# First batch's q and k loaded by head pair, its value rows held back, and PSUM banks taken as they come free, in a planned attention and feed-forward kernel

## The chip, the cores and the metric

The kernel runs on one core of a Trainium2 chip. The metric is the device time of one execution in microseconds, as the median of three runs. The core's engines are called PE (TensorE: matmuls and transposes into PSUM), DVE (VectorE), ACT (ScalarE), POOL (GpSimd, which here casts a few tiles and issues most loads) and SP (SyncE, which here only issues DMAs). PSUM, PE's output memory, has eight banks of 128 partitions by 512 float32.

## The reference

The first half is sparse attention over 8 batches, 8 heads, 576 positions and 64 values per head. The first four heads attend to a local band of 32 positions, the other four to every 32nd position. The second half is a feed-forward layer over 4608 tokens of 512 values with 2048 hidden units.

```python
scores = (1.0 / np.sqrt(D)) * np.matmul(q, k.transpose(0, 1, 3, 2))
rel = pos[:, None] - pos[None, :]
mask_local = (rel >= 0) & (rel < 32)
mask_strided = (rel >= 0) & (pos[None, :] % 32 == pos[:, None] % 32)
scores = np.where(masks[None], scores, -1000000000.0)   # heads 0-3 local, 4-7 strided
attn = softmax(scores)
x = np.matmul(attn, v).transpose(0, 2, 1, 3).reshape(B * S, H * D)
h = x @ w_in
r = np.maximum(h, 0.0)
out = (s * (r * r) + b) @ w_out
```

## The kernel before, in words

**Tiles.** In a batch, attention works on four pairs of heads, `(b, m)`: `m` 0 and 1 are local (six tiles of 96 positions), `m` 2 and 3 strided (eight tiles of 72). A pair's steps on PE are: transposes of q and k into PSUM (`trans`, L405 for local pairs of the first two batches, L413 otherwise), from where ACT or DVE copies them to `qD_loc`, `kT_loc`, `qD_str`, `kTs`; scores (L533, in the first batch with a mask matmul L530 ahead of each); exponentials on ACT (L551); products with v (`av`, L590); a reciprocal and a multiplication into `x_nat` (L605, L616, or L611 on ACT); transposes of `x_nat` (L638) and a copy of them into `xT`. Pairs of heads share one index `mm = m % 2`, so `ql` and `kl`, the tiles of the local heads, hold pair 0 in their first half and pair 1 in their second.

**Feed-forward.** Tokens go in nine blocks `T` of 512. `ff1` (called F1 below, L883) makes 16 hidden tiles per block with four matmuls each, one per `xT` tile `ct`; ACT or DVE apply relu and square into `gT`; `ff2` (L941, and `ff2_seven`, L851, from block 3 on) multiplies by `w_out`. F1 of block 0 needs all four pairs of batch 0 and `w_in`.

**Who orders what.** The whole program is recorded by a planner before it is built: `Plan` keeps a clock `t`, a free time per engine and a table of when each thing is expected to be there. PE's steps are recorded in the order in which the planner thinks them ready; posted jobs (copies, exponentials, casts, loads) go to the engine that the planner thinks would finish them first, among those that the post names a cost for. The numbers for when loads land are written by hand. On the chip each engine works through its own list strictly in order, and waits on semaphores where the expectation was too early.

**PSUM.** The eight banks are named `t` (one), `s` (two), `a` (one), `f1` (two) and `f2` (two). `group_of` deals the banks' tags out to transposes (`t`), scores (`s`) and products (`a`) by a fixed rotation, and inside a tag a step takes the next bank in turn, so that it waits for exactly that bank. Where PE would have nothing to do in the head of the kernel, `keep_running` records filler matmuls (L1177).

**Loads of the first batch.** POOL issues, one after the other: `ql`, `kl` (288 KB each as stored), `qs`, `ks`, `vs` (each in two pieces of 64 and 8 rows). SP issues the identity, two pieces of the local heads' v (`stage_v`, L240, one piece of 144 KB per head, float32, into a part of `w_out_sb` that is not yet used), and the mask addends `negs`. Then SP waits: `after_landing` issues a copy of one element of `ql` (L1051), which must wait for the landing of `ql`, and behind it in SP's list stand the v pieces of heads 2 and 3, the masks and two scalars. POOL casts the v pieces to float16 into `v_loc` (`cast_v`, two casts per pair of heads), copies 32 rows of them (`rows_before`), and only then, behind a small copy that waits for `qs` (L1069), issues the three pieces of `w_in` (L307, 2 MB). Behind these in POOL's list stand the casts for heads 2 and 3, the first piece of `w_out` (L313), the next batch's q and k, the rest of `w_out`, and the next batch's v.

Of the kernel before, what the change touches and what calls it, by code (L numbers as in the profile page):

```python
# [9 lines left out]
FP16 = mybir.dt.float16  # L10
FP32 = mybir.dt.float32
# [4 lines left out]
class Plan:  # L16
# [9 lines left out]
    def __init__(self):  # L26
        self.t = 0.0
        self.done = {}
        self.pend = []
        self.free = {"A": 0.0, "V": 0.0, "P": 7000.0, "D": 0.0, "X": 0.0, "Y": 0.0}  # L30
        self.count = {}

    def ready_at(self, needs):
        if any(k not in self.done for k in needs):
# [6 lines left out]
    def flush(self):  # L41
        while True:
            best = None
            for p in self.pend:
                r = self.ready_at(p[0])
                if r is not None and r <= self.t and (best is None or r < best[0]):
                    best = (r, p)
            if best is None:
                return
            r, p = best  # L50
            self.pend.remove(p)
            eng = min(p[1], key=lambda e: max(self.free[e], r) + p[1][e])
            end = max(self.free[eng], r) + p[1][eng]
            self.free[eng] = end
            p[2](eng)
            for k in p[3]:
                if isinstance(k, Group):
                    k = ("rel", k.tag, k.n)
                soon = isinstance(k, tuple) and k[0] == "soon"
                self.done[k] = end + (6000.0 if soon else p[4] or self.LAT[eng])  # L60

    def step_ready(self, s):
        r = self.ready_at(s.needs)
        if r is None:
# [47 lines left out]
def kernel(  # L112
# [17 lines left out]
    PS = 512  # L130
# [115 lines left out]
    nc.vector.memset(part32, 1.0 / 32)  # L246
    nc.vector.memset(vl_stage[0:LPAD], 0.0)
    for i in range(2):
        nc.vector.memset(qD_loc[i], 0.0)
        nc.vector.memset(kT_loc[i][:, 0:LPAD], 0.0)  # L250
        nc.vector.memset(qD_str[i], 0.0)
    for i in range(NV):
        nc.vector.memset(v_loc[i][:, :, :, D:D + 1], 1.0)
# [4 lines left out]
    for tl in p_bufs[False]:  # L258
        nc.vector.memset(tl[:, 16 * SQ:], 0.0)

    loaded = {}
    paired = {}

    def load_qk(b):
        for name, src in (("q", q), ("k", k)):
            tl = inp.tile([LQ, NL], FP16, tag=name + "l", name=name + "l")
            loaded[b, name + "l"] = tl
            if b >= (QB_DMA if name == "q" else KB_DMA):

                dst = tl.rearrange("p (m t e d) -> p m e t d", m=2, t=LT, e=2)  # L270
                for h in range(4):
                    nc.gpsimd.dma_start(out=dst[:, h // 2, h % 2],
                                        in_=src[b, h].rearrange("(t p) d -> p t d", p=LQ))
            else:
                nc.gpsimd.dma_start(out=h4(tl), in_=view_l(src, b))
        for name, src in (("q", q), ("k", k)):
            if name == "k":
                ts = ks[b % 2]
            elif b < QS_DMA + 2:
                ts = inp.tile([SR, NS], FP16, tag="qs", name="qs")  # L280
            else:
                ts = loaded[b - 2, "qs"]
            if name == "k" and b in (2, 3) or name == "q" and b in (QS_DMA, QS_DMA + 1):
                nc.gpsimd.memset(ts[64:SR], 0.0)
            load_s(ts, src, b)
            loaded[b, name + "s"] = ts
# [47 lines left out]
    def cast_v(b, loc, mm, key):  # L334
        nt, np_, dst = (LT, 128, v_loc) if loc else (ST, SQ, v_str)

        def g(eng):
            src = vl_stage if loc else loaded[b, "vs"].rearrange(
                "p (h t d) -> p h t d", h=4, d=D)
            for h in range(2 * mm, 2 * mm + 2):  # L340
                copy_on(eng, out=dst[b % NV][0:np_, h, :, 0:D], in_=src[:, h])
        n = nt * D
        plan.post([key], {"P": 1000.0} if loc else {"A": 2 * (170 + 0.83 * n), "V": 540.0}, g,
                  [("cast", b, mm) if loc else ("in", "vs", b, mm)])
        if loc:
            rows_before(b, mm, ("cast", b, mm))

    def rows_before(b, mm, key):
# [5 lines left out]
        def g(eng):  # L354
# [4 lines left out]
    TB, SB, AB, F1B, F2B = 1, 2, 1, 2, 2  # L359
    HEAD_T = 2  # L360
    PE_MASK = 1
    ps = {tag: [psum.tile([128, PS], FP32, name=f"ps_{tag}{i}") for i in range(n)]
          for tag, n in (("t", TB), ("s", SB), ("a", AB), ("f1", F1B), ("f2", F2B))}

    taken = {"a": 0, "t": 0, "s": 0}

    def group_of(kind, b, m, q=False):

        t, a, f1, f2 = ("t", TB), ("a", AB), ("f1", F1B), ("f2", F2B)
        banks = {"a": [a], "t": [t], "s": [("s", SB)]}[kind]  # L370
        if b == 0:
            banks = {"a": [f2, f2, f1], "t": [t, a], "s": [("s", SB), ("s", SB), f1]}[kind]
        elif b == 1 and kind == "a":
            banks = [f1, f1, a]
        elif b >= KB_DMA and kind == "a":
            banks = [a, t]
        elif b == 1 and q:
            banks = [t, f2]
        taken[kind] += 1
        return Group(*banks[taken[kind] % len(banks)])  # L380

    def bank(group):
        return ps[group.tag][group.n % group.bufs]

    def pair_steps(b, m):

# [196 lines left out]
        def av(e, j, group):  # L583
# [13 lines left out]
            if j % per == per - 1:  # L597
# [467 lines left out]
    nc.sync.dma_start(out=b_sb, in_=moe_b.to_broadcast([128, 1]))  # L1065
# [96 lines left out]
    def keep_running(until):  # L1162

        ghz = 1.2 if plan.t < 6000 else 2.4
        n = min(int((until - 100.0 - plan.t) * ghz) - 20, 512) // 128
        for tag, bufs in (("f1", F1B), ("s", SB), ("f2", F2B)):
            k = ("rel", tag, plan.count.get(tag, 0) - bufs)
            if k[2] < 0 or plan.done.get(k, until) <= plan.t:
                break
        else:  # L1170
            return False
        if n < 1:
            return False
        out = ps[tag][plan.count.get(tag, 0) % bufs][:, 0:128 * n]
# [93 lines left out]
```

## Time and profile before

| | |
|---|---|
| median of 3 runs | 307.34 us (307.26 to 307.39) |
| the profiled execution | 307.34 us, of which the span of the trace is 305.6 us |
| PE busy | 297.7 us, 97% of the span |
| DVE, ACT, POOL busy | 215.6, 183.7, 93.9 us |
| DMA moved | 37.31 MB, mean 122 GB/s |
| filler matmuls (L1177) | 9.64 us busy, all before 25 us |

PE is busy nearly throughout, and the head of the kernel is the part where some of its work is filler. Matmuls are pipelined and their ends are modelled, so busy time on PE also covers some short waits. A line with one time is a start in microseconds from the span's start; a line with two is a start and a length.

### The profile page before, as it was taken

The numbers are of one execution on the slowest core, as the hardware profiler recorded it, in microseconds if no ns is written. First come the engines' busy times: TensorE is split into PE (matmuls) and PEld (weight loads), VectorE is DVE, ScalarE is ACT, GpSimd is POOL, SyncE is SP. The second block draws the span as 40 slices with busy tenths as digits, with TensorE's granted clock in tenths as the row PEclk, the third lists the DMA queues.
The fourth block names the chain that finished last, engine by engine and source line by source line (L and its number), as shares of the span: only waits on it lengthen the run. The fifth ranks groups of instructions, "written<-read, shape, count | busy, mean of one in ns | idle before, by whom it ended". The sixth has DMA issues, their size and how long they took to land.

```text
span 305.6 us, 6880 instructions
## 1 busy us (share of the span) xinstructions
PE 297.7 (97%) x2686; PEld 206.6 (68%) x2686; DVE 215.6 (71%) x479; ACT 183.7 (60%) x330; POOL 93.9 (31%) x136
## 2 busy tenths in 40 slices
PE   8899999999999999999999999999999999999995
PEld 3775645666655567777567776778888666766884
DVE  6575857799868678449897987688765366737563
ACT  1786756698957794768397945794525444444300
POOL 7572549910980491089106830000000000000000
PEclk9999999999999999999999999999999999999999
DMA  7999999999999699999999999704010200300223
GB/s 128 207 211 206 214 160 158 197 184 148 80 156 170 73 150 132 194 150 143 125 201 141 145 141 195 167 17 127 2 36 34 71 1 34 105 0 2 84 73 121
DMA packets 100795, 37.31 MB, mean 122 GB/s; under 512 B 80874, under 2 KB 97770, under 8 KB 100762
## 3 DMA queue, kind: packets, MB, share of 16 engines
q0 software_dynamic: 57200, 18.08, 58.8%
q1 hardware_dynamic: 43562, 18.78, 31.7%
q8 instruction: 21, 0.34, 0.5%
q14 instruction: 12, 0.10, 0.1%
HBM read 36.86 MB, written 10.32 MB: 154 GB/s over the span
## 4 chain that ended last, share of the span: by engine, by line
PE 88%; DMA 8%; POOL 1%; issue 1%; ACT 1%; DVE 1%; SPq 0%; POOLq 0%
PE ps_f L883 38%; PE ps_f L851 21%; PE ps_f L941 12%; DMA ql<-in_q_dram 6%; PE ps_s L533 5%; PE ps_a L590 3%; DMA w_out_sb<-in_v_dram 2%; PE ps_s L851 2%; PE ps_t L413 2%; PE ps_t L590 1%; PE ps_t L851 1%; PE ps_s L941 1%; PE ps_t L638 1%; POOL v_loc L317 1%; PE ps_a L851 1%
## 5 line engine op out<-in xcount | busy, mean ns | idle before, releaser
L883 PE MATMUL ps_f<-xT,w_in_sb 128*128 128x512 f16 (+4 forms) x696 | 148.1, 340 | 0.1
L910 ACT ACTIVATE u<-ps_f 128x512 f16<-128x512 f32 x138 | 81.6, 596 | 73.2 <-PE ps_f L883 71.7
L883 PEld LDWEIGHTS <-w_in_sb 128*128 128x128 f16 x704 | 71.5, 113 | 32.1 <-issue 0.2
L851 PEld LDWEIGHTS <-gT 128*128 128x128 f16 x512 | 49.1, 98 | 11.5
L920 DVE TENSOR_TENSOR gT<-u 128x1024 f16<-128x1024 f16 x50 | 34.4, 688 | 24.7 <-ACT u L910 24.2
L941 PE MATMUL ps_f<-w_out_sb,gT 128*128 128x512 f16 x176 | 47.9, 379 | 0.3 <-DVE gT L920 0.3
L851 PE MATMUL ps_f<-w_out_sb,gT 128*128 128x256 f16 x312 | 43.4, 273 | 0.0
L941 PEld LDWEIGHTS <-gT 128*128 128x128 f16 x192 | 17.2, 98 | 12.3 <-DVE gT L920 0.4
L616 DVE TENSOR_TENSOR x_nat<-ps_a,rec 72x256 f16<-72x256 f32 (+1 forms) x52 | 23.8, 457 | 0.6
L551 ACT ACTIVATE p_loc<-ps_s 128x384 f16<-128x384 f32 x46 | 20.9, 493 | 5.0 <-PE ps_s L533 4.0
L918 ACT ACTIVATE gT<-u 128x1024 f16<-128x1024 f16 x22 | 23.3, 1058 | 0.6
L551 ACT ACTIVATE p_str<-ps_s 72x432 f16<-72x432 f32 (+1 forms) x46 | 20.8, 483 | 1.9 <-PE ps_s L533 1.7
L295 POOL DMA_DIRECT2D v_loc<-in_v_dram x28 | 20.7, 757 | 3.5 <-DVE qD_loc L317 1.8
L590 PEld LDWEIGHTS <-p_str 72*128 72x128 f16 x256 | 15.5, 98 | 8.8 <-issue 1.1
L723 DVE TENSOR_TENSOR gT<-gT 128x1024 f16<-128x1024 f16 x28 | 18.5, 683 | 2.6 <-ACT gT L918 1.3
L851 PE MATMUL ps_f<-w_mix,gT 128*128 128x256 f16 x144 | 18.3, 273 | 0.0
L851 PEld LDWEIGHTS <-S 128*128 128x128 f16 x160 | 15.4, 98 | 3.4
L1012 POOL COPY gate<-kT 1x1 f16<-1x1 f16 x6 | 1.9, 322 | 42.7 <-DMA kT<-ks 42.7
L605 DVE RECIPROCAL rec<-ps_a 72x4 f32<-72x4 f32 (+1 forms) x52 | 9.1, 174 | 8.3 <-PE ps_a L590 8.2
L723 DVE TENSOR_TENSOR S<-gT 128x1024 f16<-128x1024 f16 x16 | 10.6, 687 | 5.6 <-PE ps_f L851 4.5
L300 POOL DMA_DIRECT2D v_str<-in_v_dram x16 | 13.2, 828 | 3.8 <-PE ps_f L883 1.8
L851 PE MATMUL ps_f<-w_mix,S 128*128 128x256 f16 x96 | 13.7, 272 | 0.0
(156 smaller groups left out, 418.4 us busy)
## 6 DMA issues: line engine op xcount, KB each, us to landing
out_dram<-o SPq DMA_DIRECT2D x34, 256.0 KB, 2.4
w_out_sb<-in_moe_w_out_dram POOLq DMA_DIRECT2D x4, 512.0 KB, 10.8
v_loc<-in_v_dram POOLq DMA_DIRECT2D x28, 72.0 KB, 7.0
ql<-in_q_dram POOLq DMA_DIRECT2D x6, 288.0 KB, 6.3
qs<-in_q_dram POOLq DMA_DIRECT2D x6, 288.0 KB, 5.6
ks<-in_k_dram POOLq DMA_DIRECT2D x6, 288.0 KB, 6.7
kl<-in_k_dram POOLq DMA_DIRECT2D x4, 288.0 KB, 8.0
kl<-in_k_dram POOLq DMA_DIRECT2D x16, 72.0 KB, 4.0
```

What stands on the lines that cost most here:

```text
L295: nc.gpsimd.dma_start(out=vl[LPAD:128, h, :, 0:D], in_=v_band(b, h))
L533: nc.tensor.matmul(out=st["s", g][0:nk, c:c + 2 * nq], lhsT=(st["k"][:, i * nq:i * nq + nk] if loc else st["k"][:, i, 0:SQ]), rhs=st["q"][ ...
L551: nc.scalar.activation(out=st["pw", g][0:nk, 0:2 * n * nq], in_=st["s", g][0:nk, 0:2 * n * nq], func=AF.Exp, scale=scale)
L590: nc.tensor.matmul(out=st["a"][:, j % per, :], lhsT=st["pw", g][0:nk, i * nq:i * nq + WIDE], rhs=vt[0:nk, 2 * mm + e, j, :])
L616: nc.vector.tensor_tensor(out=st["x"][:, j0:j0 + per, 64 * e:64 * e + 64], in0=st["pa", e, j][0:nq, 0:per, 0:D], in1=st["rec", e, j][0:nq, ...
L723: nc.vector.tensor_tensor(out=at(out), in0=at(x), in1=at(y), op=op)
L851: nc.tensor.matmul(out=gts[name, T, t][:, 0] if halves else gts[name, T][:, t], lhsT=lhs(k, t), rhs=rhs(k), start=fresh and k == 0 and (ha ...
L883: nc.tensor.matmul(out=gts["h", T, ft][:, lo:hi], lhsT=w_in_sb[min(ft // 4, 2)][:, ct].rearrange("p (c x l) -> p c l x", x=128, l=4)[:, ma ...
L910: nc.scalar.activation(out=u, in_=gts["h", T, ft], func=AF.Relu)
L918: nc.scalar.activation(out=g, in_=u, func=AF.Square)
L920: nc.vector.tensor_tensor(out=g, in0=u, in1=u, op=ALU.mult)
L941: nc.tensor.matmul(out=gts[id_], lhsT=gts[T][:, ft, ts * 128:(ts + 1) * 128], rhs=w_out_sb[:, ft, cols], start=(ft == 0), stop=(ft == NFT ...
```

## The change

Five things change.

1. `load_qk(0)` loads the local q and k of batch 0 in four pieces, by pair of heads: q of pair 0, k of pair 0, q of pair 1, k of pair 1 (144 KB each) in place of two transfers of 288 KB.
2. SP issues `negs` ahead of v, only one piece of v (head 0) at the start, and the other three behind the one-element copy, which now reads the second half of `ql` and so waits for the third of the four pieces.
3. The order of the memsets on DVE is changed. The hand-written landing times are changed to a table `AT`.
4. The planner's cost table for the strided v cast of batch 0 names POOL too (1500 ns).
5. A `Group` now names a set of banks, and a step takes the one of them that the planner expects free first. More banks are named for transposes of batches 1 and 2, for F1 of block 0 and for the fillers. `rec` takes one pool of 8 buffers.

```diff
@@ Plan.flush, Plan.step_ready, Plan.emit, Group
-                    k = ("rel", k.tag, k.n)
+                    self.banks[k.name] = end + self.LAT[eng]
+                    k = ("rel", k)
...
-            n = self.count.get(s.group.tag, 0)
-            if n >= s.group.bufs:
-                k = ("rel", s.group.tag, n - s.group.bufs)
-                if k not in self.done:
-                    return None
-                r = max(r, self.done[k])
+            free = [self.banks[x] for x in s.group.names if self.banks[x] is not None]
+            if not free:
+                return None
+            r = max(r, min(free))
...
-            s.group.n = self.count.get(s.group.tag, 0)
-            self.count[s.group.tag] = s.group.n + 1
+            free = [x for x in s.group.names if self.banks[x] is not None]
+            s.group.name = min(free, key=lambda x: self.banks[x])
+            self.banks[s.group.name] = None
...
-    def __init__(self, tag, bufs):
-        self.tag, self.bufs, self.n = tag, bufs, None
+    def __init__(self, *tags):
+        self.names = [f"{tag}{i}" for tag, bufs in zip(tags[::2], tags[1::2]) for i in range(bufs)]
+        self.name = None
@@ the start
     nc.sync.dma_start(out=ident, in_=h_ident.ap())
-    stage_v(range(2))
     nc.sync.dma_start(out=negs, in_=h_neg.ap())
+    stage_v(range(1))
...
     def load_qk(b):
-        for name, src in (("q", q), ("k", k)):
+        for mm in range(2) if b == 0 else ():
+            hs = slice(2 * mm, 2 * mm + 2)
+            for name, src in (("q", q), ("k", k)):
+                if mm == 0:
+                    loaded[b, name + "l"] = inp.tile([LQ, NL], FP16, tag=name + "l", name=name + "l")
+                nc.gpsimd.dma_start(out=h4(loaded[b, name + "l"])[:, hs],
+                                    in_=view_l(src, b)[:, hs])
+        for name, src in (("q", q), ("k", k)) if b else ():
@@ cast_v
-        plan.post([key], {"P": 1000.0} if loc else {"A": 2 * (170 + 0.83 * n), "V": 540.0}, g,
+        plan.post([key], {"P": 1000.0} if loc else {"A": 2 * (170 + 0.83 * n), "V": 540.0,
+                                                           **({"P": 1500.0} if b == 0 else {})}, g,
@@ group_of
-        banks = {"a": [a], "t": [t], "s": [("s", SB)]}[kind]
+        banks = {"a": a, "t": t, "s": sc}[kind]
         if b == 0:
-            banks = {"a": [f2, f2, f1], "t": [t, a], "s": [("s", SB), ("s", SB), f1]}[kind]
+            banks = {"a": f2 + f1 + a, "t": t + a, "s": sc + f1}[kind]
         elif b == 1 and kind == "a":
-            banks = [f1, f1, a]
+            banks = f1 + a
...
         elif b == 1 and q:
-            banks = [t, f2]
-        taken[kind] += 1
-        return Group(*banks[taken[kind] % len(banks)])
+            banks = t + f2
+        elif b == 2 and q:
+            banks = t + f1
+        elif kind == "t" and b == 1:
+            banks = t + f1 + a
+        return Group(*banks)
@@ av
-                    st["rec", e, j] = recp.tile([128, 6, 1], FP32, tag="rec" + group.tag,
-                                                bufs=group.bufs, name="rec")
+                    st["rec", e, j] = recp.tile([128, 6, 1], FP32, tag="rec", bufs=8,
+                                                name="rec")
@@ the first batch's landing times and the held-back loads
-    for name, at in (("q", 6950.0), ("k", 8750.0)):
-        arrive(both(name + "l", 0), at)
-    arrive(both("qs", 0), 10100.0)
-    arrive(both("ks", 0), 11600.0)
-    plan.done["raw", "v", False, 0] = 13800.0
-    after_landing(0, loaded[0, "ql"][0:1, 0:1])
-    stage_v(range(2, 4))
+    plan.free["V"] = 6500.0
+    AT = {"ql0": 5300.0, "kl0": 6400.0, "ql1": 7400.0, "kl1": 8500.0, "qs": 11000.0,
+          "ks": 13000.0, "vs": 14600.0, "vl0": 9800.0, "vl1": 13000.0}
...
+    plan.done["raw", "v", False, 0] = AT["vs"]
+    after_landing(0, loaded[0, "ql"][0:1, NL // 2:NL // 2 + 1])
+    stage_v(range(1, 4))
...
-    for mm, at in (0, 7100.0), (1, 14400.0):
+    for mm, at in (0, AT["vl0"]), (1, AT["vl1"]):
@@ F1 of block 0
-            gr = [Group(*x) for x in (("s", SB), ("s", SB), ("f1", F1B), ("f1", F1B))]
+            gr = [Group("s", SB, "f1", F1B) for _ in range(4)]
...
-            gr = Group("f2", F2B) if T == 0 and ft % 4 < 2 else Group("f1", F1B)
+            gr = Group("f1", F1B, "f2", F2B) if T == 0 else Group("f1", F1B)
```

In the built program PE has 26 fillers in place of 32; on POOL two load issues are added; the four strided v copies of batch 0 stand on DVE (two) and ACT (two), as before; two copies of q of batch 0 (a local and a strided pair's) go from DVE to ACT and one copy of k goes from ACT to DVE; and 41 F1 matmuls stand ahead of the second batch's first transposes, where there were 36. The order of all later steps is drawn anew by the planner.

More of the change, by code (lines that the diff above doesn't have):

```diff
@@ L30, in __init__ @@
         self.free = {"A": 0.0, "V": 0.0, "P": 7000.0, "D": 0.0, "X": 0.0, "Y": 0.0}
-        self.count = {}
+        self.banks = {}
     def ready_at(self, needs):
@@ L242 @@
     nc.sync.dma_start(out=ident, in_=h_ident.ap())
-    stage_v(range(2))
     nc.sync.dma_start(out=negs, in_=h_neg.ap())
+    stage_v(range(1))
     nc.vector.memset(ones16, 1.0)
-    nc.vector.memset(part32, 1.0 / 32)
-    nc.vector.memset(vl_stage[0:LPAD], 0.0)
     for i in range(2):
@@ L250 @@
         nc.vector.memset(kT_loc[i][:, 0:LPAD], 0.0)
+    nc.vector.memset(vl_stage[0:LPAD], 0.0)
+    for i in range(2):
         nc.vector.memset(qD_str[i], 0.0)
@@ L259 @@
         nc.vector.memset(tl[:, 16 * SQ:], 0.0)
+    nc.vector.memset(part32, 1.0 / 32)
     loaded = {}
@@ L361 @@
     PE_MASK = 1
-    ps = {tag: [psum.tile([128, PS], FP32, name=f"ps_{tag}{i}") for i in range(n)]
-          for tag, n in (("t", TB), ("s", SB), ("a", AB), ("f1", F1B), ("f2", F2B))}
-    taken = {"a": 0, "t": 0, "s": 0}
+    ps = {f"{tag}{i}": psum.tile([128, PS], FP32, name=f"ps_{tag}{i}")
+          for tag, n in (("t", TB), ("s", SB), ("a", AB), ("f1", F1B), ("f2", F2B)) for i in range(n)}
+    plan.banks.update({name: 0.0 for name in ps})
     def group_of(kind, b, m, q=False):
-        t, a, f1, f2 = ("t", TB), ("a", AB), ("f1", F1B), ("f2", F2B)
-        banks = {"a": [a], "t": [t], "s": [("s", SB)]}[kind]
+        t, a, f1, f2, sc = ("t", TB), ("a", AB), ("f1", F1B), ("f2", F2B), ("s", SB)
+        banks = {"a": a, "t": t, "s": sc}[kind]
         if b == 0:
-            banks = {"a": [f2, f2, f1], "t": [t, a], "s": [("s", SB), ("s", SB), f1]}[kind]
+            banks = {"a": f2 + f1 + a, "t": t + a, "s": sc + f1}[kind]
         elif b == 1 and kind == "a":
-            banks = [f1, f1, a]
+            banks = f1 + a
         elif b >= KB_DMA and kind == "a":
-            banks = [a, t]
+            banks = a + t
         elif b == 1 and q:
-            banks = [t, f2]
-        taken[kind] += 1
-        return Group(*banks[taken[kind] % len(banks)])
+            banks = t + f2
[4 more added lines that the diff above has]
+        return Group(*banks)
     def bank(group):
-        return ps[group.tag][group.n % group.bufs]
+        return ps[group.name]
     def pair_steps(b, m):
@@ L1055 @@
     plan.free["P"] = 7100.0
-    for name, at in (("q", 6950.0), ("k", 8750.0)):
-        arrive(both(name + "l", 0), at)
-    arrive(both("qs", 0), 10100.0)
-    arrive(both("ks", 0), 11600.0)
-    plan.done["raw", "v", False, 0] = 13800.0
-    after_landing(0, loaded[0, "ql"][0:1, 0:1])
-    stage_v(range(2, 4))
+    plan.free["V"] = 6500.0
+    AT = {"ql0": 5300.0, "kl0": 6400.0, "ql1": 7400.0, "kl1": 8500.0, "qs": 11000.0,
+          "ks": 13000.0, "vs": 14600.0, "vl0": 9800.0, "vl1": 13000.0}
+    for key, at in AT.items():
+        if key[:2] == "vl":
+            continue
+        arrive([("in", key[:2], 0, mm) for mm in range(2) if key[2:] in ("", str(mm))], at)
+    plan.done["raw", "v", False, 0] = AT["vs"]
+    after_landing(0, loaded[0, "ql"][0:1, NL // 2:NL // 2 + 1])
+    stage_v(range(1, 4))
     nc.sync.dma_start(out=masks, in_=h_mask.ap())
@@ L1165, in keep_running @@
         n = min(int((until - 100.0 - plan.t) * ghz) - 20, 512) // 128
[L1166 to L1170, printed above, removed]
+        free = [x for x in plan.banks if x[0] in "fs" and plan.banks[x] is not None
+                and plan.banks[x] <= plan.t]
+        if not free:
             return False
@@ L1173, in keep_running @@
             return False
-        out = ps[tag][plan.count.get(tag, 0) % bufs][:, 0:128 * n]
+        out = ps[free[0]][:, 0:128 * n]
         def f():
```

## The prediction

> **What bounds the kernel now.** I read the page first, its slices and its chain of waits. PE is busy in every slice, at a granted clock of 9 or more tenths.
>
> ```profile
> PE 297.7 (97%) x2686; PEld 206.6 (68%) x2686; DVE 215.6 (71%) x479; ACT 183.7 (60%) x330; POOL 93.9 (31%) x136
> PE   8899999999999999999999999999999999999995
> PE 88%; DMA 8%; POOL 1%; issue 1%; ACT 1%; DVE 1%; SPq 0%; POOLq 0%
> ```
>
> PE carries 88% of the chain, and the matmuls are the same in both kernels. So time can only change by what PE loses: fillers (9.64 us, all before 25 us) and waits. The chain in order of time shows what the lost head is made of (start, length):
>
> ```profile
> 1.27 5.84 DMA ql<-in_q_dram
> 7.13 0.76 SPq L1051
> 7.94 6.52 DMA w_out_sb<-in_v_dram
> 14.59 0.58 POOL v_loc L317
> 15.20 0.52 POOL v_loc L317
> 15.77 0.73 POOL v_loc L317
> ...
> 17.32 12.11 DMA ql<-in_q_dram
> 29.47 0.45 PE ps_f L405 x12
> ```
>
> The first batch's q lands, SP's one-element copy follows, the held-back v pieces land 6.5 us after their issue, POOL casts them, and the second batch's q is issued. This is the chain that the change edits. What else hangs on the v casts is in POOL's timeline, where 10.68 is the issue of `w_in`:
>
> ```profile
> 6.26 0.58 POOL L317 CAST v_loc<-w_out_sb 128x384 f16<-128x384 f32 x1
> 7.39 1.29 POOL L317 CAST v_loc<-w_out_sb 128x384 f16<-128x384 f32 x2 [0.55 <-DMA w_out_sb<-in_v_dram]
> 10.45 0.18 POOL L1069 COPY gate<-qs 8x1 f16<-8x1 f16 x1 [1.77 <-DMA qs<-in_q_dram]
> 10.68 2.29 POOL L307 DMA_DIRECT2D w_in_sb<-in_moe_w_in_dram  x3
> 14.59 1.90 POOL L317 CAST v_loc<-w_out_sb 128x384 f16<-128x384 f32 x3 [1.61 <-DMA w_out_sb<-in_v_dram]
> ```
>
> Today the casts of heads 0 and 1 end at 8.68, ahead of the landing of `qs`, and cost nothing. Last, the transfers issued before 16 us (KB each, us to landing), where DMA moves 195 to 240 GB/s without a pause from 4.5 us on:
>
> ```profile
> w_out_sb<-in_v_dram SPq DMA_DIRECT2D x4, 144.0 KB, 6.3
> ql<-in_q_dram POOLq DMA_DIRECT2D x1, 288.0 KB, 5.8
> kl<-in_k_dram POOLq DMA_DIRECT2D x1, 288.0 KB, 6.8
> qs<-in_q_dram POOLq DMA_DIRECT2D x1, 256.0 KB, 7.4
> ks<-in_k_dram POOLq DMA_DIRECT2D x1, 256.0 KB, 7.6
> vs<-in_v_dram POOLq DMA_DIRECT2D x1, 256.0 KB, 8.7
> ```
>
> With their issues at 1.27, 2.11, 2.79, 3.96 and 5.11 these land at 7.1, 8.9, 10.2, 11.6 and 13.8. Undisturbed, 288 KB take 1.4 us.
>
> **The parts.** The sum is made against the profiled execution: 307.34, span 305.6, so 1.74 outside the span; it equals the median.
>
> *Local q and k.* 144 KB of v no longer run ahead of them: 0.7 us at 1.4 per 288 KB. So k of pair 1 lands at 8.2, and the pieces before it 0.7 apart: 7.5 (q of pair 1), 6.8, 6.1. POOL issues four pieces: whole tiles cost 0.71 to 0.84, the smallest load issue in the trace 0.53, so I take 0.62 each; 2.5 in place of 1.55 pushes `qs`, `ks` and `vs` back by 0.95 on POOL, hidden under data that comes 7 us or more after issue (0.95 if uncovered). Fillers of 0.43 us end at 6.2. ACT's copy of q (1.28) runs from 6.7 to 8.0, of k (0.64) to 8.6, of the other q, moved here from DVE (1.28), to 9.9, then exponentials: they start 1.3 us before today's 11.19. The second pair needs k at 8.2, behind the first pair's scores, and DVE's copy (0.76): its exponentials end about 12.6 against 13.76. So the first gain is 1.1 us, if v is there.
>
> *The held-back v.* The piece of head 1 now stands behind the one-element copy. That waits for 7.5; v follows 0.81 later (7.13 to 7.94), at 8.3. Its landing, L, decides the rest. Nearest row: the piece issued at 7.94 landed 6.65 us later (cast at 14.59), behind the same queue of `qs`, `ks`, `vs`: L = 14.95. From below: 2.4 us, the median of all output stores, most of them on idle queues: L = 10.7. In the trace the held-back pieces land about when `vs` does, after 13.8; with 144 KB fewer ahead of it `vs` ends near 12.4, and v right behind it: I take L = 13.5.
>
> [...]
>
> *What waits on it, DMA.* POOL is in order: cast 0.58, rows 0.73, the copy 0.18 and gaps put `w_in` at L + 1.6 = 15.1, against 10.68. The first packets of an idle queue came 1.7 us after issue (issue at 1.27; half the DMA share in 1.5 to 3 us): 16.8. The other bytes after `kl` (864 KB of strided tiles, 288 KB of v, 42 KB of masks, 1194 KB at 200 a us from 8.0) are out at 14.0. So DMA, which today goes straight on, stands still for 2.8 us, and the second batch's q, 10 us of `w_in` and `w_out` later, lands at 32.2 in place of 29.4.
>
> *What waits on it, ACT.* PE's list has the products of pair 0 ahead of five transposes of `qs` and all of `ks`, so the strided pairs also wait for L + 1.4. Then 0.55 (12 products), 0.3 (transposes), and on ACT from its timeline: q 1.28 (moved from DVE), k 0.64, v 1.14, exponentials 1.23 and 1.35, `x_nat` 0.91, `xT` 0.64, `x_nat` 0.91, `xT` twice 0.64, less 0.7 of overlap: 8.7. The last `xT` is there at L + 10.9 = 24.4; today 22.20 + 0.64 = 22.84. That is 1.6 us lost on PE. The 41 F1 matmuls ahead of the second batch, 25 of them after the first 16 (at 0.216), end near 31.0, and PE then waits 1.2 us for 32.2, against 0.35 today: 0.85 more.
>
> *Who stands behind these waits.* On POOL behind the second cast: the copy, `w_in`, the casts for heads 2 and 3, `w_out` and the second batch's loads. On SP behind the one-element copy: v, the masks (first read by DVE at 37.7, so covered) and two scalars. On PE behind the products of pair 0: the strided transposes, then all strided scores; on DVE their reciprocals, ahead of a copy of k and the v casts.
>
> *Banks.* The waits view for PE has two waits for a bank outside the head:
>
> ```profile
> PE ps_f L413 <- ACT kT_loc L317: 0.7, 1, 0.7
> PE ps_a L590 <- DVE x_nat L616: 0.4, 1, 0.4
> ```
>
> So -1.1 at best; a newly drawn order can also lose that. I take -0.4. Memsets, `rec` and the table cost nothing on the chip but that order. The strided v cast's new engine is not taken: worth 0.
>
> Sum: +1.6 +0.85 -0.4 = +2.05, 309.4 us. At L = 14.95: DMA 4.2, ACT 3.1, together about +3.4 less 0.4, and up to 0.9 more if every later load stays late: 311.2. At L = 10.7 neither path is late: below.
>
> **The rivals.** *Faster: v lands early.* If L is 10.9 or less, `w_in` data follow without a pause and ACT is set by its own work: exponentials end at 12.6, v and `vs` do not hold it, 8.7 us and small waits end at 22.0, 0.8 before today. Less 0.4 at banks, plus 0.2 more waiting for the second batch's q, which stays at 29.4: 306.3. For it: the gate opens while little of `qs` is left. Against it: 6.52 us. *No change: the new order pays.* PE's starts, less each matmul's usual step, show four gaps after 30 us: 0.94 at 32.2, 0.7 near 44.5, 1.0 near 85 and 0.3 at 220.6. If all go, -2.9 in place of -0.4 leaves -0.45: 306.9. Against it: only 1.1 of these are waits for a bank. *No effect.* Part 4 does nothing; the others are in the built program, so this one has no time of its own. *Slower still: late loads.* If L is 15 and the second batch's v, behind the same DMA stream, arrives after PE wants it, PE pays all 4.2 us: 311.5.
>
> **The numbers.** The forecast with the late case: 0.70 together (0.60 and 0.10). No change to within 0.2% (0.6 us, about what a measurement of this kernel can tell): 0.08, with L near 11.5 or banks that pay. Faster: 0.22. Eight in ten lies between 306.2, the early landing, and 311.3, the late one; slower cases alone span 308.1 to 311.3.
>
> **What would show it.** Right: `w_in` issued after 14 us, POOL waiting several us for `w_out_sb` before its second cast, a hole in DMA's GB/s near 15 us, the second batch's q landing after 31. The exponentials should start near 10 us. Wrong: the second cast by 11 us and no hole; or the hole, and a second batch that starts no later than 29.5; or a loss that sits after 60 us.

## The result, and the profile after

The changed kernel took 312.28 us (median of 6 runs, 310.97 to 314.32) against 307.44 for the kernel before in the same comparison: ratio 1.0158 (95%: 1.0121 to 1.0195), 4.8 us slower. Run again, on the chip of experiments 13 to 16, it was 1.0102 (1.0082 to 1.0123), 311.77 against 308.75: 3.0 us. The forecast, 309.4, was 1.0067 of before. The kernel before took 307.44 us in the comparison of the result and 308.7 to 309.1 us on the four chips of the runs below, so kernels are compared by their ratio to it, or within one chip.

The profiled execution after is 310.97 us, span 309.2: 3.63 us more than the one before. The page's slices (7.73 us each), PE, granted clock and DMA:

```profile
PE   8599999999989999999999999999999999999995
PEclk9959999999999999999999999999999999999999
DMA  8999999999999899979998999924010300300123
```

Before, PE's second slice was an 8 and every PEclk digit a 9. Now PE is half idle in the second slice, and in the third it has half its clock. The chain of waits in the head, in order of time (start, length), shows why PE idles:

```profile
2.70 4.61 DMA ql<-in_q_dram
7.33 0.77 SPq L1064
8.15 5.71 DMA w_out_sb<-in_v_dram
13.91 0.52 POOL v_loc L327
14.48 0.73 POOL v_loc L327
15.25 0.52 PE ps_f L603 x11
```

It is the chain shown of before, with head 1 in place of head 2: q of pair 1 lands, SP's copy follows, the held-back v is 5.7 us under way, POOL casts it. Before, the next link was a DMA issue; now PE's products of pair 0 hang on it. POOL's timeline (start, busy, in brackets the idle time before and its releaser):

```profile
13.91 1.29 POOL L327 CAST v_loc<-w_out_sb 128x384 f16<-128x384 f32 x2 [5.88 <-DMA w_out_sb<-in_v_dram]
15.26 0.18 POOL L1085 COPY gate<-qs 8x1 f16<-8x1 f16 x1
15.38 2.29 POOL L317 DMA_DIRECT2D w_in_sb<-in_moe_w_in_dram  x3
20.43 0.69 POOL L285 DMA_DIRECT2D ql<-in_q_dram  x1
```

POOL waits 5.88 us for the piece of head 1, and `w_in` is issued at 15.38 in place of 10.68, though the gate copy that it is meant to wait for could run at 9.6. PE, from its waits (line waited for, total, times, longest):

```profile
PE ps_f L603 <- POOL v_loc L327: 3.0, 1, 3.0
```

And stretches of 3 us, with busy time and count of PE, PEld, DVE, ACT and POOL, then granted clock, DMA share and GB/s:

```profile
12.00:15.00 3.00, 0.24 (x8) 0.15 (x5) 0.91 (x2) 0.48 (x2) 1.03 (x2) 1.00 1.02 154
15.00:18.00 3.00, 2.61 (x36) 2.06 (x36) 1.28 (x4) 1.88 (x4) 2.90 (x6) 0.61 0.25 19
18.00:21.00 3.00, 3.00 (x29) 2.93 (x27) 1.23 (x4) 2.40 (x6) 2.64 (x5) 0.50 1.23 204
21.00:24.00 3.00, 3.00 (x49) 2.83 (x48) 1.74 (x8) 1.69 (x5) 2.93 (x6) 0.75 1.21 211
```

Three things are to be seen: PE nearly without work from 12 to 15, DMA nearly without work (19 GB/s) from 15 to 18, and the clock at a half from 15.7 to 22.5. DMA's hole was forecast, and PE's wait follows from what the prediction says of PE's list; the fall of the clock was not forecast.

### The profile page after: what moved, and what is told of

It is laid out like the page before. It is cut to its first block, busy times and chain, and to the rows that moved or that the text cites. A ratio compares the mean times of both kernels' runs of the same rounds, so it can differ in the third digit from the quotient of the medians.

```text
span 309.2 us, 6827 instructions
## 1 busy us (share of the span) xinstructions
PE 299.5 (97%) x2680; PEld 208.2 (67%) x2680; DVE 214.1 (69%) x477; ACT 186.5 (60%) x332; POOL 94.5 (31%) x138
## 3 DMA queue, kind: packets, MB, share of 16 engines
q1 hardware_dynamic: 43562, 18.78, 30.3%
## 4 chain that ended last, share of the span: by engine, by line
PE 91%; DMA 3%; DVE 2%; POOL 1%; ACT 1%; issue 1%; SPq 0%; DVEq 0%; POOLq 0%
PE ps_f L896 38%; PE ps_f L864 20%; PE ps_f L954 12%; PE ps_s L546 5%; PE ps_a L603 3%; DMA w_out_sb<-in_v_dram 2%; PE ps_s L864 2%; DMA ql<-in_q_dram 1%; PE ps_t L426 1%; PE ps_t L603 1%; PE ps_t L864 1%; PE ps_s L954 1%; PE ps_t L651 1%; PE ps_f L603 1%; DVE qD_str L327 1%
## 5 line engine op out<-in xcount | busy, mean ns | idle before, releaser
L933 DVE TENSOR_TENSOR gT<-u 128x1024 f16<-128x1024 f16 x46 | 31.5, 685 | 20.9 <-ACT u L923 20.2
L931 ACT ACTIVATE gT<-u 128x1024 f16<-128x1024 f16 x26 | 27.5, 1057 | 0.8
L629 DVE TENSOR_TENSOR x_nat<-ps_a,rec 72x256 f16<-72x256 f32 (+1 forms) x55 | 25.2, 458 | 0.7
L564 ACT ACTIVATE p_str<-ps_s 72x432 f16<-72x432 f32 (+1 forms) x45 | 20.0, 484 | 3.3 <-PE ps_s L546 3.3
L736 DVE TENSOR_TENSOR gT<-gT 128x1024 f16<-128x1024 f16 x28 | 18.7, 684 | 3.5 <-PE ps_f L864 2.1
L618 DVE RECIPROCAL rec<-ps_a 72x4 f32<-72x4 f32 (+1 forms) x55 | 9.8, 178 | 14.7 <-PE ps_a L603 14.4
L327 ACT COPY qD_loc<-ps_t 64x576 f16<-64x576 f16 x18 | 11.4, 632 | 4.5 <-PE ps_t L418 3.4
```

Source lines behind the costliest of these rows:

```text
L564: nc.scalar.activation(out=st["pw", g][0:nk, 0:2 * n * nq], in_=st["s", g][0:nk, 0:2 * n * nq], func=AF.Exp, scale=scale)
L629: nc.vector.tensor_tensor(out=st["x"][:, j0:j0 + per, 64 * e:64 * e + 64], in0=st["pa", e, j][0:nq, 0:per, 0:D], in1=st["rec", e, j][0:nq, ...
L736: nc.vector.tensor_tensor(out=at(out), in0=at(x), in1=at(y), op=op)
L931: nc.scalar.activation(out=g, in_=u, func=AF.Square)
L933: nc.vector.tensor_tensor(out=g, in0=u, in1=u, op=ALU.mult)
```

## The experiments

Theory: the held-back v is the loss, by POOL's wait, the DMA hole and PE's wait, and, once the profile after had shown it, by the clock. Rival: the new order of PE and choice of banks is the loss, and the held-back v lies beside other work.

**1. The hold undone.** SP issues two pieces at the start; only SP's list differs from the changed kernel.

```diff
-    stage_v(range(1))
+    stage_v(range(2))
...
-    stage_v(range(1, 4))
+    stage_v(range(2, 4))
```

> The changed kernel with one thing undone: the v pieces of heads 0 and 1 are both issued at the start, as before, and only those of heads 2 and 3 stand behind the one-element copy. Every engine's list but SP's stays as in the changed kernel. Theory (the held-back v is the loss: POOL waits for it, w_in is issued 5 us late, PE waits 3.0 us at 12.0 and its clock falls to half): w_in issued near 10.5 to 11, no DMA hole, no half clock after 12 us, the second batch's q near 29.4, and a time of 306 to 307.7. Rival (the new PE order and choice of banks are the loss, and the held-back v lies beside other work): the time stays at 311 to 312.5, though w_in is issued early.

Ratio 0.996 (0.9947 to 0.9973); profiled 306.99 us, clock 1.0, `w_in` issued at 10.33, the second batch's q landed at 30.3 (expected near 29.4). The stretch in which the changed kernel had its hole:

```profile
15.00:18.00 3.00, 2.81 (x57) 2.77 (x55) 2.12 (x7) 3.00 (x8) 2.64 (x5) 1.00 1.00 149
```

The rival falls: with the new order and banks but early v, the kernel is faster than before.

**2. The hold alone, on the kernel before.**

```diff
-    stage_v(range(2))
+    stage_v(range(1))
...
-    stage_v(range(2, 4))
+    stage_v(range(1, 4))
```

> The kernel before with that one thing done: only the v piece of head 0 is issued at the start, the piece of head 1 stands behind the one-element copy. Every engine's list but SP's stays as before. Theory (held-back v): the piece lands near 14, POOL waits about 6 us before its second cast, w_in is issued near 15.5, the second batch's q lands near 33, and the time is 310 to 312.5, the upper end if PE's wait also drops its clock. Rival (the new order is the loss): 307 to 308, no more than 0.5 us above before.

Ratio 1.0086 (1.0063 to 1.0109), 2.4 us above before. `w_in` at 15.00, the second batch's q at 32.6, PE without work for 2.7 us from 12.1, clock at a half from 15.4 to 18.8. The hold does damage of the same kind in the old order, 2.4 us; in the new order it is 4.0 us (experiments 13 and 14).

**3. Fillers in the wait.** They change no other engine's list.

```diff
                 if j % per == 0:
+                    if (b, m, e, j) == (0, 0, 0, 0):
+                        for _ in range(14):
+                            nc.tensor.matmul(out=bank(group)[:, 0:512], lhsT=ones16,
+                                rhs=ones16[:, None, :].to_broadcast([128, 4, 128]),
+                                start=True, stop=True)
```

> The changed kernel with 14 more filler matmuls (128x512 of ones, 3.0 us at full clock, into the bank of the first products) ahead of the first products, where PE waits for v. They change no wait of another engine: they only keep PE busy in its 3.0 us wait. Theory (the idle PE lost its clock, which stretched everything from 15 to 22.5 us): the granted clock stays at 0.95 or more in 15 to 24 us, and the time falls by 1 to 2.5 us, to 309.5 to 311. Rival (the clock is no part of the loss, PE waits for ACT and DMA anyway): same time to within 0.5 us, 311.5 to 313.

Ratio 1.0062 (1.0036 to 1.0089). In its profile (310.37 us) the clock stays full through the head, while DMA's hole is still there:

```profile
15.00:18.00 3.00, 1.99 (x38) 1.48 (x37) 1.40 (x5) 1.94 (x4) 2.89 (x6) 1.00 0.27 26
```

Among seven runs five have 0.998 or more, two 0.994 and 0.989. The size is taken from one chip, in experiments 13 to 16.

**4. `w_in` first on POOL.** The gate copy and the three issues of `w_in` are moved ahead of the v casts; all other lists stay.

```diff
             src = vl_stage if loc else loaded[b, "vs"].rearrange(
                 "p (h t d) -> p h t d", h=4, d=D)
+            if b == 0 and loc and mm == 0:
+                nc.gpsimd.tensor_copy(out=gate[0:8, 2:3], in_=loaded[0, "qs"][64:SQ, 0:1])
+                load_w_in()
```

> The changed kernel with POOL's list alone reordered: the one-element copy of qs and the three issues of w_in come ahead of the v casts. The held-back v and PE's wait for it stay. Theory: w_in is issued near 10, the DMA hole of 3 us near 16 is filled and the second batch's q lands near 30 in place of 33.2; PE still waits for v (to 15 or a little later, since w_in now shares DMA with it) and still loses its clock, so about 1 us comes back if PE would have waited for q, or nothing if the clock had used that time up: 310.5 to 312.3. Rival (DMA's late start is the whole loss): 307 to 308.5. Rival (new order): 311.5 to 312.5.

Ratio 1.0166 (1.0137 to 1.0194): nothing comes back, and 314.06 us lies above the 310.5 to 312.3 that were expected. `w_in` was issued at 10.07 and the hole is filled, as its stretches show:

```profile
15.00:18.00 3.00, 1.54 (x27) 1.37 (x27) 1.19 (x4) 0.74 (x2) 2.44 (x5) 0.82 1.29 199
```

But the earlier traffic pushes v back: head 1 is cast at 15.11 in place of 13.91, and PE waits till 16.4. The second batch's q lands at 31.70, 1.5 us earlier, with nobody to use it, since PE gets to its transposes at 36.1. So DMA's hole alone isn't what sets the time; PE's own head is as late.

**5 and 6. One part alone on the kernel before, v early in both.** In 5 the planner's banks, `group_of`, F1's groups and `rec` of the diff, of which the core is

```diff
-        if s.group is not None:
-            s.group.n = self.count.get(s.group.tag, 0)
...
+            s.group.name = min(free, key=lambda x: self.banks[x])
...
-            banks = {"a": [f2, f2, f1], "t": [t, a], "s": [("s", SB), ("s", SB), f1]}[kind]
+            banks = {"a": f2 + f1 + a, "t": t + a, "s": sc + f1}[kind]
```

> The kernel before with the bank part alone: banks taken as they come free, the wider choice of banks, and the new rec buffers; loads, due times, casts and v as before. Theory (the prediction's bank term, -0.4 us, bounds -1.1 to +0.5): ratio 0.996 to 1.002, no half clock. If the changed kernel without the held-back v gains its 0.4% from the banks alone, this shows 0.996 and the next one 1.000.

In 6 the loads by head pair with their due times and casts:

```diff
-        for name, src in (("q", q), ("k", k)):
+        for mm in range(2) if b == 0 else ():
...
+    AT = {"ql0": 5300.0, "kl0": 6400.0, "ql1": 7400.0, "kl1": 8500.0, "qs": 10100.0,
+          "ks": 11600.0, "vs": 13800.0, "vl0": 9800.0, "vl1": 13000.0}
```

> The kernel before with the load part alone: q and k by head pair with their due times, and the gate on q of pair 1, but the v pieces of heads 0 and 1 still issued at the start; banks as before, and the strided tiles' due times as before, without which the old planner finds no order. Theory (the prediction's load term: exponentials about 1 us earlier, end hidden by the rest of the head): exponentials start near 10, ratio 0.996 to 1.000. If the banks alone make the gain, 1.000 or above.

Banks alone: 1.0049 (1.0027 to 1.0071). Loads alone: 1.0034 (1.0012 to 1.0055). Both are slower, where the two together, experiment 1, are faster. In 5 PE's starts show a gap of 1.7 us at 192 us and gaps of 3.1 us between 75 and 90; in 6 there are 3.0 us between 61 and 88. The kernel before has 1.0 there. So most of what is lost is lost far from the head. Both expectations were wrong: each part draws a new order for the whole kernel, worth 1 to 1.5 us in either direction here, and such terms do not add up.

**7. Early v, with the due times that the trace shows.**

```diff
-    AT = {"ql0": 5300.0, "kl0": 6400.0, "ql1": 7400.0, "kl1": 8500.0, "qs": 11000.0,
-          "ks": 13000.0, "vs": 14600.0, "vl0": 9800.0, "vl1": 13000.0}
+    AT = {"ql0": 5800.0, "kl0": 7000.0, "ql1": 7700.0, "kl1": 8700.0, "qs": 10100.0,
+          "ks": 11600.0, "vs": 13500.0, "vl0": 6300.0, "vl1": 14600.0}
```

> The changed kernel with v of heads 0 and 1 early (as in the first experiment, 0.996 of before) and the planner's due times set to the landings that its trace shows: q and k of the pairs 5.8, 7.0, 7.7 and 8.7, qs 10.1, ks 11.6, vs 13.5, v 6.3 and 14.6. Only the order of the lists changes. Theory: v is no wait any more, so the order around it is worth little: 0.994 to 0.998, a gain of at most 0.6 us over the first experiment. Rival (the order drawn for late v is a loss of its own): 0.992 or less.

Ratio 0.994 (0.9919 to 0.9962): at the edge of what the theory expected. The intervals of 1 and 7 overlap, so this run alone doesn't show a gain over experiment 1.

**8. v of head 1 through POOL's own queue,** behind the four pieces of q and k.

```diff
-    def stage_v(heads):
+    def stage_v(heads, eng=nc.sync):
...
+        if b == 0:
+            stage_v(range(1, 2), nc.gpsimd)
...
-    stage_v(range(1, 4))
+    stage_v(range(2, 4))
```

> The changed kernel with v of head 1 issued not by SP behind the one-element copy but by POOL, behind the four pieces of local q and k and ahead of qs. Lists as in the changed kernel but for this one transfer. Theory (the piece is late because it waits for the copy and then shares DMA with everything that POOL has queued): it lands near 9, behind q and k of pair 1, the second cast is near 9.5, w_in is issued near 11, PE does not wait at 12 and keeps its clock, and the time is 0.994 to 0.998 of before: 144 KB stand no longer ahead of the local q and k, but 0.35 us more ahead of the strided tiles. Rival (any v piece that isn't issued at the start is late): it lands after 12 and the ratio is 1.005 or more.

It landed at 9.64, in its turn, and PE's wait for v was gone. But the ratio is 1.0002 (0.9978 to 1.0026), not 0.996: the strided tiles and then `w_in` were pushed back (issued at 11.35, landed at 20.07 against 18.62 in experiment 1), and PE waited there instead:

```profile
PE ps_s L898 <- DMA w_in_sb<-in_moe_w_in_dram: 1.7, 1, 1.7
```

The clock then fell in some runs and not in others. Of 12 runs three kept 1.0 (307.10 to 307.65 us), seven had 0.993 to 0.994 (307.95 to 310.32), two 0.988 (309.98, 310.23). The medians of the three groups are 307.53, 308.99 and 310.11: in runs of one kernel on one chip, each step down of the clock goes with 1.1 to 1.5 us. The three runs that kept it are at 0.996 of before, as the theory expected. That speaks for the clock, more than the wait for `w_in` by itself, as what this version lost.

**9. The second batch's q and k ahead of the first chunk of `w_out`,** on top of 7.

```diff
-        weights_out(range(1))
         fetch_qk(1)
-        weights_out(range(1, 4))
+        weights_out(range(4))
```

> The best version so far (v of heads 0 and 1 early, due times set to the measured landings; 0.994 of before) with one more edit: POOL issues the second batch's q, k and strided tiles ahead of the first chunk of w_out instead of behind it. In its trace PE waits 0.9 us for that q (landed 30.9) and 0.6 us for k, and w_out's first chunk is first read at 39.9. Theory (PE's head is held by the DMA stream, as the prediction's DMA term has it): q lands 1 to 1.5 us earlier, those waits go, and the ratio is 0.989 to 0.993. Rival (what is saved there comes back as a later wait, for the strided tiles or w_out): 0.993 to 0.997.

Ratio 0.993 (0.9902 to 0.9957). q lands at 27.6 in place of 30.9 and PE's two waits there (0.77 us for q and 0.46 for k in the trace of 7) are gone, yet the intervals of 7 and 9 overlap: whether it pays by itself stays open.

**10. Half the fillers:** 7 in place of 14.

> The changed kernel with 7 filler matmuls in PE's wait for v in place of the 14 of the earlier experiment (14 gave a clock of 1.0 in most runs and 1.006 of before, none gives 0.984 to 0.989 and 1.016). PE now idles about 1.5 us in one piece. If the clock falls only when PE is idle for some 3 us in one piece, the result is that of 14: 1.005 to 1.008. If it is the share of idle time in a window that decides, some runs lose one or two half-clock stretches of 3.4 us and others none: a spread of clocks from 0.989 to 1.0 and a ratio of 1.008 to 1.013.

Ratio 1.0047 (1.0028 to 1.0066); with 14 it was 1.0062 and 1.0069, on other chips. PE was without work for 2.1 us in its profile (from 13.7) and for 0.7 at 17.1, and the clock was down from 18.7 to 22.1; of ten runs six kept 0.998 or more, three had 0.993 to 0.994, one 0.989. So behind waits of this size some runs lost the clock and others kept it. The ratio is nearer the first theory's, the spread of clocks is the second's.

**11. An earlier gate.** SP's copy reads q of pair 0.

```diff
-    after_landing(0, loaded[0, "ql"][0:1, NL // 2:NL // 2 + 1])
+    after_landing(0, loaded[0, "ql"][0:1, 0:1])
```

> The changed kernel with SP's one-element copy reading q of pair 0 (landed 5.2) instead of pair 1 (7.3): the held-back v is issued near 6.2 instead of 8.15, every list unchanged. By the prediction's reading (v lands behind what POOL has queued, about when vs does, whenever it is issued) it lands at 13 or later, PE still waits over 2 us, and the ratio is 1.010 to 1.016. By the other reading (v gets its share of DMA at once, and its landing follows its issue) it lands 2 us earlier, near 11.9 or before, and the ratio is 0.997 to 1.003.

Ratio 1.011 (1.0088 to 1.0131). The chain of waits of this run:

```profile
5.73 0.76 SPq L1064
6.54 7.60 DMA w_out_sb<-in_v_dram
14.19 0.52 POOL v_loc L327
```

Issued 1.6 us earlier than in the changed kernel (6.54 against 8.15), v lands no earlier (14.1 against 13.9). On the chip of this run experiments 10 and 12, with the gate of the changed kernel, had it at 14.4 and 14.7, so the earlier issue brought 0.3 to 0.6 us. As the prediction read it, v lands behind `vs`: at 14.5 against 14.1 in the kernel before, at 13.9 against 13.2 in the changed one.

The packets show that this isn't all due to the end of POOL's queue. After v's issue the queue of SP's transfers moves nothing for 3.3 to 3.4 us (7.94 to 11.26 in the kernel before, 8.15 to 11.51 in the changed one), while POOL's moves 0.67 and 0.63 MB, 202 and 187 GB/s. After that the two run side by side: before, SP's moves 0.34 MB and POOL's 0.36 from 11.25 to 14.5; in the changed kernel SP's moves 0.17 and POOL's its last 0.07 from 11.5 to 12.5, and then SP's goes on alone, 0.29 MB to 14.0. What holds the first packet back isn't shown, and a run with the piece of head 1 alone at that place was not made.

**12. One more filler** of 512 columns just after PE's wait.

```diff
+        extra = len(count) == 22
...
         def f():
+            if extra:
+                nc.tensor.matmul(
+                    out=whole, lhsT=ones16, rhs=ones16[:, None, :].to_broadcast([128, 4, 128]),
+                    start=True, stop=True)
```

> The changed kernel with one more filler matmul (128x512; 0.43 us at half clock) just after the wait for v, where PE waits 0.44 us for a bank while its clock is down (16.7 us). Nothing else changes. In the changed kernel the clock stays down for 6.8 us, two stretches of 3.4; in the kernel before with v held back, where PE has no such wait, it is down for 3.4. Theory (a stretch with a wait of that size in it does not bring the clock back): the clock is back after one stretch, 0.994, and the ratio falls from 1.016 to 1.010 to 1.012. Rival (the length is set by the idle time before it, or by chance): clocks of 0.984 to 0.989 and 1.015 to 1.017 as without it.

The clock is 0.987 to 0.989 in five of six runs and down for 6.8 us in the profile, as without it, though PE is now busy all through the first of the two steps, 17.0 to 20.4: the theory that a small wait keeps the clock down falls. The ratio, 1.0072 (1.0046 to 1.0098), met neither expectation; it looked like a gain against the changed kernel's 1.0158, while its interval overlaps that of the repeat, 1.0102. That is why the changed kernel was run again beside its variants.

**13 to 16. All terms on one chip.** In this order: the changed kernel (13), the kernels of experiments 1 (14) and 3 (15), and that of 9 (16).

> The changed kernel itself, unchanged, on the same chip as the next three. The kernel before took 307.4, 308.7 and 309.1 us on the chips of the other comparisons, so ratios from different chips may not be subtracted. Theory (v held back: wait and DMA hole 3 us, half clock 2 to 3 us, less 1 us from loads and banks): ratio 1.010 to 1.017, every run at a clock of 0.984 to 0.989.

> The changed kernel with v of heads 0 and 1 early, as in the first experiment, beside the changed kernel on one chip: the difference is all that holding v back costs. Theory: 4.5 to 6 us below the changed kernel, ratio 0.995 to 0.998 of before. If the first experiment's gain came from its chip, 0.998 to 1.002 here.

> The changed kernel with 14 fillers in the wait for v, beside the changed kernel on one chip: the difference is the clock's share, what is left above the kernel with v early is the wait's and the DMA hole's. Theory: 2 to 3 us below the changed kernel, 2.5 to 3.5 us above the one with v early. Rival (the clock's share is small, the first figure came from different chips): within 1 us of the changed kernel.

> The best version (v early, due times set to the measured landings, second batch's q and k ahead of the first w_out chunk) on the same chip: 0.991 to 0.995 of before, 0.3 to 1.5 us below the one with v early alone.

| kernel | median us | ratio to before (308.75) |
|---|---|---|
| changed | 311.77 | 1.0102 (1.0082 to 1.0123) |
| changed, fillers in the wait | 310.89 | 1.0069 (1.0047 to 1.0091) |
| changed, v early | 307.81 | 0.997 (0.9952 to 0.9988) |
| v early, measured due times, q and k first | 306.43 | 0.9926 (0.9907 to 0.9945) |

Loads and banks together are worth -0.9 us (307.81 - 308.75), the wait and what hangs on it +3.1 (310.89 - 307.81), the clock +0.9 (311.77 - 310.89). The hold as a whole costs 4.0 us, less than the 4.5 to 6 expected. The clock's share is less than the 2 to 3 us expected, and by the medians it is what the rival said (within 1 us); the intervals of the two kernels overlap, so the medians alone show it weakly. Part of the reason is that the filler kernel loses its clock too in three of its six runs. Its three runs at 0.999 or more have a median of 310.23 and all lie below every run of the changed kernel, which makes the share 1.5.

The last row beats both kernels: 2.3 us below the one before. Its page's slices, with no weak slice in the head:

```profile
PE   8999999999999999999999999999999999999995
PEclk9999999999999999999999999999999999999999
```

## Why the prediction missed

The direction and the chain were right, the size was too small: +2.05 us forecast, +4.8 in the result, +3.0 when it was run again.

*Local loads.* Forecast to land at 6.1, 6.8, 7.5 and 8.2, they landed at 5.16, 6.25, 7.31 and 8.12; the exponentials began at 9.52 (forecast 9.9).

*The held-back v.* L was put at 13.5 between bounds of 10.7 and 14.95; it was 13.9, and 13.9 to 14.7 in experiments 3, 10, 12, 13 and 15, which issue it behind q of pair 1 too. No run shows the L near 11.5 that the chance of no change names: in these it was 13.9 or later. In the changed kernel the first packet came 3.4 us after the issue, and not after the 1.7 that the prediction took for first packets, and SP's queue then shared DMA with the end of POOL's (0.17 and 0.07 MB from 11.5 to 12.5).

*POOL and DMA.* `w_in` was forecast at 15.1 and issued at 15.38; the hole is there (19 GB/s in 15 to 18), and the second batch's q, forecast at 32.2, landed at 33.2.

*ACT's path: here the size was off.* The last `xT` was forecast at L + 10.9 = 24.4. With the clock kept (experiment 3) it was there at 26.0, L + 12.1: 1.2 us more than the list of durations held, of which two waits of ACT that the list left out, 0.31 us for scores and 0.64 for transposes, make 0.95. In the changed kernel it was there at 28.06: 2.06 us more again, since the clock was down. ACT's timeline shows what the clock does, gaps before the exponentials where ACT waits for scores, five with 1.90 us in all against the one of 0.31 in experiment 3. The last three:

```profile
21.39 0.53 ACT L564 ACTIVATE p_str<-ps_s 72x432 f16<-72x432 f32 x1 [0.31 <-PE ps_s L546]
22.55 0.53 ACT L564 ACTIVATE p_str<-ps_f 72x432 f16<-72x432 f32 x1 [0.64 <-PE ps_f L546]
23.43 0.41 ACT L564 ACTIVATE p_str<-ps_s 72x288 f16<-72x288 f32 x1 [0.35 <-PE ps_s L546]
```

*PE's wait for the second batch's q.* Forecast as 0.85 us more behind ACT's 1.6: F1 ends near 31.0, q lands at 32.2, and the later of the two counts. In the changed kernel the other one was the later: q landed at 33.2, PE came to its transposes at 34.9 and never waited for it. With fillers q was the later one again, as forecast, and PE waited for it 0.24 us in experiment 3 (transposes at 33.1) and 0.41 in experiment 15 (33.3). So the clock put PE's path 1.6 us behind q, which is the size of what the profiled run has beyond the forecast: 3.63 - 2.05 = 1.58.

*Banks.* -0.4, counted from two waits. The right measure would have been the whole order: banks alone 1.0049, loads alone 1.0034, both 0.996.

*The faster rival* had its total right: v early, 306.3 us or 0.9966 of before; measured 0.996 and 0.997. That is luck in part, since its parts were not: the last `xT` was to be there at 22.0 and the second batch's q at 29.4, and in experiment 1 they were there at 23.26 and 30.3, later than before (22.84 and 29.43). The difference between rival and forecast, 3.1 us for the hold, is what experiments 14 and 15 show with fillers (3.1), and here the main part agrees too: q 2.8 us later by forecast (29.4 to 32.2), 2.8 between experiments 1 and 3 (30.3 to 33.1). The filler kernel came to 1.0062 and 1.0069, the forecast's 1.0067.

*The step that failed* is the first one: "the matmuls are the same in both kernels. So time can only change by what PE loses: fillers (9.64 us, all before 25 us) and waits." The prediction read the clock of before ("9 or more tenths"), took it over for the changed kernel and so put the clock's term at nothing; it did not ask what 3 us without work or fillers do to the clock. The same matmuls took longer behind PE's wait: at half clock for 6.83 us of the profile, which puts PE 1.6 us behind q. In experiments 13 to 16 that missing term, 0.9 to 1.5 us, is as large as the whole difference between +3.0 and the forecast's +2.05. In the result another 1.8 us (4.8 - 3.0) is unexplained. Of it, 1.3 lies in the kernel before, which ran faster there (307.44 against 308.75), and 0.5 in the changed one (312.28 against 311.77); its runs at the same clock of 0.989 go from 310.97 to 314.32, and only the fastest has a trace. This stays open.

## What to carry to other kernels

A wait on the engine that carries the chain can cost twice, as PE's did here: its length (with what hangs on it, 3.1 us), and what the engine loses of its clock behind it (0.9 to 1.5). Gaps of up to 0.94 us in the kernel before and one of 1.7 us in experiment 5 cost no clock (1.00 in the stretches around them); behind waits of 1.7 us (experiment 8) and 2.1 us (experiment 10) nine of 12 and four of ten runs lost it, so full speed behind such a wait should not be counted on. With none of the 14 fillers in the wait of 3.0 to 3.3 us all 12 runs lost it (the result and experiment 13), with them five of 13 did (3 and 15). Of terms that lie side by side, such as a late DMA stream and a late chain of copies, the later counts, and what stretches one can hide the other: in the changed kernel q landed at 33.2 and PE came to it at 34.9. A change that makes a planner draw a new order has a term of its own, of either sign (banks alone 1.0049, loads alone 1.0034, both 0.996). Here a piece of 144 KB issued at 8.15, while POOL's queue had 0.70 MB more to move, landed at 13.9, behind that work, and issuing it 1.6 us earlier hardly helped (14.1); in POOL's queue ahead of that work it landed at 9.64 (experiment 8).

## What the runs showed of the hardware

**The half clock lasted one, two or three times 3.41 us.** Summing the lost clock over stretches of 0.1 us, it lasted 3.41 us (the profiles of experiments 2 and 10), 6.83 (the changed kernel, experiments 4, 8 and 12) and 10.24 (experiments 11 and 13). The mean clocks of the runs follow: 3.41/2 us of 309 is 0.0055, and they read 0.994, 0.989 and 0.984. Gaps of 1.7 us (experiment 8), 2.1 (10), 2.7 (2) and 3.0 us (the changed kernel) were followed by half a clock, the first two only in part of the runs (nine of 12 and four of ten).

**How much of a step PE was without work before a fall.** Laying steps of 3.41 us end to end from the places where the clock changes, PE was without work for 0.42 to 0.88 of the step just before each fall (0.88 in the changed kernel, 12.26 to 15.67; 0.49 in experiment 8, 17.59 to 21.00). Of the full-speed steps with no fall behind them one had 0.45 (experiment 10, the step before the one with 0.42), and those of the changed kernel from 2.0 to 305.8 had at most 0.25. So the share does not tell a fall in every case. The gap of 1.7 us in experiment 5 was followed by no fall (clock 1.00 from 100 to 200 us).

**How long the clock stays down.** Experiment 12 rules out the one small wait. What decides isn't shown. In the changed kernel 27 of the 39 matmuls in the first step at half clock were transposes (15.67 to 19.09) and none of the 36 in the second (19.09 to 22.50), after which the clock came back. No run tested whether that matters.

**One kernel, two sizes of loss.** The same changed kernel was 1.0158 of before in the result and 1.0102 when it was run again; the intervals overlap by a hair (1.0121 and 1.0123 are their near ends), and the chip of the result is not on record. Ratios from different comparisons should not be subtracted at the level of half a per cent.
